# An attention and MoE kernel: the gates of all heads, the warm-up products and the splitting of x moved in the order

## The chip, the cores and the metric

The kernel runs on one core of one Trainium2 chip. The metric is the device time of one execution in microseconds (us), lower is better. Five engines work side by side, each through its own instructions in order: TensorE (PE, with its weight loads PEld), VectorE (DVE), ScalarE (ACT), GpSimd (POOL) and SyncE (SP), which here issues all the DMA transfers.

## What is computed

Eight batches of eight heads of causal attention with decaying gates, over 576 positions of 64 features; its output, 4608 tokens of 512 features, goes through a two-layer network:

```python
scores = scale * np.matmul(q, k.transpose(0, 1, 3, 2))
log_f = np.log(np.clip(f, 0.0001, 1.0))
cum = np.cumsum(log_f, axis=-1)
decay = cum[:, :, :, None] - cum[:, :, None, :]
scores = np.where(causal, -1000000000.0, scores + decay)      # causal: above the diagonal
attn = np.exp(scores - np.max(scores, axis=-1, keepdims=True))
attn = attn / (np.sum(attn, axis=-1, keepdims=True) + 1e-09)
x = np.matmul(attn, v)                 # then heads are put side by side: (4608, 512)
h = x @ w_in                           # (4608, 2048)
sp = np.maximum(h, 0.0) + np.log1p(np.exp(-np.abs(h)))
out = (h * erf(sp)) @ w_out            # (4608, 512)
```

All inputs and the output are float32.

## The kernel before

**Attention** runs in half steps t = 0 to 63, two for each pair of heads p = t // 2; a half step has some of the pair's blocks of 128 query rows (two in even half steps, three in odd ones), for both heads j = 0, 1. The work of a half step is spread over the following ones, so in the loop's step t stand `scores(t)`, `reduce(t)`, `exps(t - 1)`, `normalize(t - 2)`, `transposes(t - 3)` with `evacuate(t - 3)`, `values(t - 4)` and `store(t - 5)`. One half step takes about 4.9 us.

- `scores(t)` multiplies q and k on TensorE into one PSUM tile for each head, and adds a mask by products with `eye`. The pool `ps_s` has two buffers, which are the two tiles of one half step: `scores(t)` writes head j's only when `reduce(t - 1, j)` has read it.
- `reduce(t, j)` on DVE adds the gate row `c` of the pair (the negative running sum of the log gates, in all 128 partitions) and takes the row minimum of what is then the negated score.
- `exps` runs on ScalarE, `normalize` on GpSimd (from sums that DVE inverts), the copies out of PSUM in `evacuate` on ScalarE (banks 0 and 1) and DVE (banks 2 and 3). The pool `ps_t` of the transposes has three buffers, so that the fourth bank of an odd half step waits until bank 0 is emptied by ScalarE.
- `store` writes the pair's output, transposed, to the DRAM tensor `xt_d`.

**The gate rows.** Those of the first pair are worked out from two broadcast loads, `fd[0]` and `fd[1]`: `log_clipped` clips on DVE (L324) and takes the logarithm on ScalarE (L325), `decay` scans (L329) and multiplies by -8 (L330) on DVE. For all other pairs, `all_decays` does the same once with `fr`, all 64 heads in 64 partitions, writes the result to the DRAM tensor `cum_d` (L482) and loads the next pairs with q, k and two rows of `cum_d` broadcast to 128 partitions (L344). It is called at the end of half step 0.

**Constant products.** `idle_products` (L472 to L476) transposes the identity into a PSUM bank that nobody reads: 16 times before the loop, and 18 times behind the scores of t = 0, 1 and 2.

**Weights.** From t = 4 on each half step does one of four conversion steps of a weight piece (`convert`), spread over ScalarE, DVE and GpSimd.

**MoE.** `Moe.step` j does the first layer for one unit (a chunk of 512 tokens by 128 hidden features: `up`, 12 products), the second layer for a unit some steps back (`down`), and the gate functions of others. The first four steps are interleaved with the last half steps of the attention; the rest runs alone. The tokens of a chunk come from `xt_d` in two halves. `want_x(v)` allocates the tiles `xh` and `xl` of visit v and queues its halves, `load_x` starts the load of the next queued half into `xr` (L113), which has one buffer, and `split_x` splits the loaded ones: ScalarE copies to `xh` (L120), GpSimd subtracts for `xl` (L121). In the kernel before, the first chunk's halves are loaded and split in t = 60 and t = 61.

**What sets the order.** ScalarE, TensorE, DVE and GpSimd take their instructions as the code writes them (`manual_schedule` of the four). SP's are ordered by the scheduler when the program is built, so a load can stand well ahead of its place in the code; SP then works through its list in order, and a transfer that must wait holds those behind it.

Of the kernel before, what the change touches and what calls it, by code (L numbers as in the profile page):

```python
# [11 lines left out]
F32 = mybir.dt.float32  # L12
# [55 lines left out]
class Moe:  # L68
# [138 lines left out]
    def step(self):  # L207
        j, n = self.at, len(self.units)
        self.at += 1
        if j < n:  # L210
            self.up(j)
            self.want_x(self.units[min(j + 4, n - 1)][0])
            self.load_x()
        for i in self.downs[j]:
            self.down(i)
        if j in self.ends:
            for i in self.ends[j]:
                self.erf(i)
            self.nc.scalar.preload_act_table_set(SOFTPLUS)
        if j < n:  # L220
            self.softplus(j)
        for i in self.gates[j]:
            self.gate(i)
        for i in self.downs[j]:
            self.finish(i)
        self.split_x()


@with_exitstack
def attention_moe(ctx, tc, q2, k2, vp, f, w_in, w_out, out):  # L230
    nc = tc.nc
# [83 lines left out]
    with ExitStack() as ph:  # L315
# [7 lines left out]
        def log_clipped(x):  # L323
            nc.vector.tensor_scalar(out=x, in0=x, scalar1=1e-4, scalar2=1.0, op0=ALU.max, op1=ALU.min)  # L324
            nc.scalar.activation(out=x, in_=x, func=AF.Ln)  # L325

        def decay(out, x):

            nc.vector.tensor_tensor_scan(out=out, data0=x, data1=x, initial=0.0, op0=ALU.add, op1=ALU.bypass)  # L329
            nc.vector.tensor_scalar(out=out, in0=out, scalar1=-8.0, scalar2=None, op0=ALU.mult)  # L330
# [3 lines left out]
        def load(p):  # L334

            q = io.tile([P, PAD + S], F32, name=f"q{p}", tag="q")
            k = io.tile([P, S], F32, name=f"k{p}", tag="k")
            nc.sync.dma_start(out=q, in_=q2[p // NP, p % NP])
            nc.sync.dma_start(out=k, in_=k2[p // NP, p % NP])
            c = io.tile([P, 2, S], F32, name=f"c{p}", tag="c")  # L340
            if p:
                for j in range(2):
                    n = 2 * p + j
                    nc.sync.dma_start(out=c[:, j], in_=cum_d[n:n + 1].rearrange("a s -> (a s)").partition_broadcast(P))  # L344
            pairs[p] = [q, k, c]
# [117 lines left out]

        fd = [wk.tile([P, S], F32, name=f"fd{j}", tag=f"pt{j}", bufs=1) for j in range(2)]
        nc.sync.dma_start(out=fd[0], in_=f[0, 0].partition_broadcast(P))
        load(0)
        nc.sync.dma_start(out=fd[1], in_=f[0, 1].partition_broadcast(P))
        fr = wk.tile([B * H, S], F32, name="fr", tag="xo")
        nc.sync.dma_start(out=fr, in_=f.rearrange("b h s -> (b h) s"))
        todo = pieces[1]  # L470

        def idle_products(t, n):  # L472
# [2 lines left out]
            for i in range(n):  # L475
                nc.tensor.transpose(out=b[:, i % 4 * P:(i % 4 + 1) * P], in_=ident, identity=ident)  # L476

        def all_decays():
            log_clipped(fr)
            cum = wk.tile([B * H, S], F32, name="cum", tag="xo")  # L480
            decay(cum, fr)
            nc.sync.dma_start(out=cum_d, in_=cum)  # L482
            load(1)
            load(2)
            load_weight(0)

        idle_products("", 16)
        log_clipped(fd[0])
        decay(pairs[0][2][:, 0], fd[0])
        log_clipped(fd[1])  # L490
        for t in range(NH + 5):
            there = [0 <= t - n < NH for n in range(6)]
# [30 lines left out]
                exps(t - 1, 1)  # L523
            if there[0]:
                reduce(t, 1)
                if t == 0:
                    all_decays()
            if there[3]:
                for a in range(1, len(BANKS[(t - 3) % 2])):
                    evacuate(t - 3, a)  # L530
            if t >= 4 and todo:
                convert(*todo.pop(0))
            if NH - 4 <= t < NH - 2:
                moe.want_x(0)
                moe.load_x()
                moe.split_x()
            if t == NH - 1:
                early.close()
                moe.ep = moe_pools.enter_context(tc.tile_pool(name="ep", bufs=2, side="right"))
# [47 lines left out]
```

## Time and profile before

| | us |
|---|---|
| median of 3 runs | 1155.87 |
| lowest and highest run | 1155.82, 1157.66 |
| the profiled execution | 1156.91 |
| its span in the trace | 1155.1 |
| TensorE busy in the span | 1134.1 |
| ScalarE, DVE, GpSimd busy | 624.4, 565.2, 461.1 |

The span is what the trace covers of the profiled execution; 1.8 us lie around it. Busy times of TensorE overstate its work a little, since its products overlap and their ends are modelled. A row of the order of time gives the start and the length of an instruction, or of several alike in a row (x16), its engine, line and operation, the tiles that it writes and reads, and in brackets how long the engine stood before it and what ended that. A product of float32 operands appears as two instructions.

### The profile page before, as it was taken

What the parts mean: (1) busy time and instruction counts of PE and PEld (TensorE: products, weight loads), DVE (VectorE), ACT (ScalarE), POOL (GpSimd) and SP (SyncE); (2) the same over time, 40 slices, a digit from 0 to 9 for tenths busy, and PEclk for the clock granted to TensorE, in tenths of its full rate; (3) what the DMA queues carried; (4) which work ended last, traced back from release to release, by engine and by line L of the source; (5) the groups of instructions that cost most, each with busy time, mean ns of one, the idle gap of its engine ahead of it and who ended that gap; (6) DMA issues with size and microseconds to landing.
All of it is one profiled execution on the core that took longest, in us unless ns stands there. A gap on an engine that the chain in (4) does not pass through costs nothing.

```text
span 1155.1 us, 19541 instructions
## 1 busy us (share of the span) xinstructions
PE 1134.1 (98%) x7334; PEld 927.9 (80%) x7334; DVE 565.2 (49%) x1475; ACT 624.4 (54%) x1251; POOL 461.1 (40%) x532
## 2 busy tenths in 40 slices
PE   8999999999989999999999999999999999999998
PEld 6888888888877878778888888888888888888886
DVE  5788888888846576565233132222321322322221
ACT  3878878787786565664444344433342443243342
POOL 2556565555654445344342342332232232232121
PEclk9999999999999999999999999999999999999999
DMA  7677777777622133131031130230010010000001
GB/s 261 206 241 258 243 231 253 237 243 234 198 98 92 54 111 108 57 113 70 19 110 40 71 110 19 91 110 1 37 37 1 37 37 1 37 19 1 37 1 37
DMA packets 57726, 120.05 MB, mean 104 GB/s; under 512 B 4768, under 2 KB 20128, under 8 KB 57632
## 3 DMA queue, kind: packets, MB, share of 16 engines
q1 hardware_dynamic: 57632, 118.80, 31.4%
q8 instruction: 58, 0.95, 0.3%
q14 instruction: 36, 0.29, 0.1%
HBM read 94.52 MB, written 24.26 MB: 103 GB/s over the span
## 4 chain that ended last, share of the span: by engine, by line
PE 90%; DVE 3%; DMA 3%; ACT 2%; POOL 1%; issue 1%; SPq 0%; POOLq 0%; DVEq 0%; ACTq 0%
PE ph L133 32%; PE y L169 11%; PE y L171 11%; PE y L170 11%; PE s L362 8%; PE o L444 8%; PE t L417 7%; PE s L367 2%; DMA wraw<-in_w_in_dram 1%; POOL xl L121 1%; DVE pr L383 1%; DMA k<-in_k_dram 0%; DVE e L147 0%; ACT L289 0%; ACT L141 0%
## 5 line engine op out<-in xcount | busy, mean ns | idle before, releaser
L133 PE MATMUL ph<-xh,w 128*128 128x512 f32 x1152 | 381.7, 392 | 5.7 <-DVE e L147 5.7
L150 POOL TENSOR_TENSOR gl<-e,gh 128x512 fp32r<-128x512 f32 x144 | 186.8, 1298 | 418.9 <-DVE gh L149 414.4
L138 ACT ACTIVATE e<-ph 128x512 f32<-128x512 f32 x144 | 86.1, 598 | 385.1 <-PE ph L133 380.3
L133 PEld LDWEIGHTS ph<-xh,w 128*128 128x128 f32 x1152 | 217.2, 189 | 56.6 <-DVE e L147 5.9
L147 DVE TENSOR_TENSOR e<-e,ph 128x512 f32<-128x512 f32 x144 | 98.1, 681 | 327.0 <-ACT e L141 326.8
L169 PE MATMUL y<-w,gh 128*128 128x512 f32 x576 | 228.9, 397 | 0.0
L171 PE MATMUL y<-w,gl 128*128 128x512 f32 x576 | 228.0, 396 | 0.0
L170 PE MATMUL y<-w,gh 128*128 128x512 f32 x576 | 227.6, 395 | 0.0
L133 PE MATMUL ph<-xl,w 128*128 128x512 f32 x576 | 225.4, 391 | 0.0
L405 POOL TENSOR_SCALAR pr<-pr,st 128x576 f32<-128x576 f32 (+4 forms) x320 | 164.7, 535 | 117.8 <-DVE st L401 102.0
L395 ACT ACTIVATE pr<-pr,st 128x576 f32<-128x576 f32 (+3 forms) x320 | 176.5, 556 | 3.6 <-DVE st L383 3.5
L383 DVE CUSTOM_DVE_ANT_0 pr<-s,c 128x576 f32<-128x576 f32 (+3 forms) x320 | 136.8, 487 | 52.6 <-PE s L367 39.2
L171 PEld LDWEIGHTS y<-w,gl 128*128 128x128 f32 x576 | 108.7, 189 | 27.0
L170 PEld LDWEIGHTS y<-w,gh 128*128 128x128 f32 x576 | 108.2, 188 | 26.1
L169 PEld LDWEIGHTS y<-w,gh 128*128 128x128 f32 x576 | 108.0, 188 | 24.4
L133 PEld LDWEIGHTS ph<-xl,w 128*128 128x128 f32 x576 | 108.4, 188 | 22.7
L149 DVE CAST gh<-e 128x512 fp32r<-128x512 f32 x144 | 92.2, 640 | 66.3 <-PE y L170 52.4
L362 PE MATMUL s<-k,q 64*128 64x320 f32 (+4 forms) x768 | 110.3, 411 | 4.5 <-DVE st L383 2.5
L417 PE MATMUL t<-ident,pr 128*128 128x128 f32 x800 | 103.9, 275 | 4.2 <-ACT pt L426 2.5
L426 ACT COPY pt<-t 128x512 f32<-128x512 f32 x128 | 73.7, 577 | 61.1 <-PE t L417 61.1
L444 PE MATMUL o<-pt,v 128*64 128x128 f32 (+1 forms) x1920 | 103.8, 261 | 0.0
L444 PEld LDWEIGHTS o<-pt,v 128*64 128x64 f32 x1920 | 94.9, 138 | 9.5 <-DVE st L383 4.9
(53 smaller groups left out, 992.2 us busy)
## 6 DMA issues: line engine op xcount, KB each, us to landing
v<-in_vp_dram SPq DMA_DIRECT2D x32, 576.0 KB, 6.2
c<-cum_d SPq DMA_DIRECT2D x62, 288.0 KB, 5.0
xr<-xt_d SPq DMA_DIRECT2D x28, 512.0 KB, 3.4
q<-in_q_dram SPq DMA_DIRECT2D x32, 320.0 KB, 3.2
k<-in_k_dram SPq DMA_DIRECT2D x32, 288.0 KB, 4.2
xt_d<-xo SPq DMA_DIRECT2D x32, 288.0 KB, 5.8
wraw<-in_w_in_dram SPq DMA_DIRECT2D x16, 512.0 KB, 5.8
wraw<-in_w_out_dram SPq DMA_DIRECT2D x16, 512.0 KB, 5.6
```

The costliest lines, as they stand in the source:

```text
L133: nc.tensor.matmul(out=ps, lhsT=w[:, kd, fs], rhs=x[:, kd], start=kd == 0 and n == 0, stop=kd == KD - 1 and n == 2)
L147: nc.vector.tensor_mul(e_, e_, h_)
L150: nc.gpsimd.tensor_tensor(out=gl, in0=e_, in1=gh.bitcast(F32), op=ALU.subtract)
L169: nc.tensor.matmul(out=y[tb], lhsT=gh[:, cs], rhs=wh, start=first, stop=False)
L170: nc.tensor.matmul(out=y[tb], lhsT=gh[:, cs], rhs=wl, start=False, stop=False)
L171: nc.tensor.matmul(out=y[tb], lhsT=gl[:, cs], rhs=wh, start=False, stop=last)
L362: nc.tensor.matmul(out=s[j][:, at:at + k1 - k0], lhsT=q[h, PAD + START[i]:PAD + END[i]], rhs=k[h, k0:k1], start=i > 0, stop=k1 < END[i])
L383: nc.vector.tensor_tensor_reduce(out=to[:, ::-1] if j else to, in0=score, in1=decay_, scale=-0.125, scalar=BIG, op0=ALU.add, op1=ALU.min, ...
L395: nc.scalar.activation(out=seg, in_=seg, func=AF.Exp, bias=st[:, 0, j, m:m + 1], scale=-1.0, accum_out=st[:, 1, j, m:m + 1])
L405: nc.gpsimd.tensor_scalar(out=seg, in0=seg, scalar1=st[:, 2, j, m:m + 1], scalar2=1.0, op0=ALU.mult, op1=ALU.mult)
L417: nc.tensor.transpose(out=b[:, n * P:(n + 1) * P], in_=probs[t][:, at:at + P], identity=ident)
L444: nc.tensor.matmul(out=o[h, to:to + width], lhsT=v[:, ch, h], rhs=pt[:, at[j]:at[j] + width], start=n == 0, stop=n == len(parts) - 1, skip ...
```

## The change

The load of `fr` is issued right behind that of `fd[0]`, ahead of the first q and k. The function `all_decays` is gone: its clip and logarithm stand behind those of `fd[0]`, its scan and multiply behind the first head's, and the write to `cum_d` with the loads behind it follows, all before the loop. The first constant products are 34 in place of 16. The first chunk of x is asked for in t = 54, 57 and 60: each time the half that is loaded is split, and then the next load is started. In `Moe.step` the load comes behind the split at the step's end, and the next chunk is asked for one step earlier.

```diff
@@ Moe.step
         if j < n:
             self.up(j)
-            self.want_x(self.units[min(j + 4, n - 1)][0])
-            self.load_x()
+            self.want_x(self.units[min(j + 5, n - 1)][0])
...
         self.split_x()
+        self.load_x()
@@ attention_moe
         nc.sync.dma_start(out=fd[0], in_=f[0, 0].partition_broadcast(P))
+        fr = wk.tile([B * H, S], F32, name="fr", tag="xo")
+        nc.sync.dma_start(out=fr, in_=f.rearrange("b h s -> (b h) s"))
         load(0)
         nc.sync.dma_start(out=fd[1], in_=f[0, 1].partition_broadcast(P))
-        fr = wk.tile([B * H, S], F32, name="fr", tag="xo")
-        nc.sync.dma_start(out=fr, in_=f.rearrange("b h s -> (b h) s"))
...
-        def all_decays():
-            log_clipped(fr)
-            cum = wk.tile([B * H, S], F32, name="cum", tag="xo")
-            decay(cum, fr)
-            nc.sync.dma_start(out=cum_d, in_=cum)
-            load(1)
-            load(2)
-            load_weight(0)
-
-        idle_products("", 16)
+        idle_products("", 34)
         log_clipped(fd[0])
+        log_clipped(fr)
         decay(pairs[0][2][:, 0], fd[0])
+        cum = wk.tile([B * H, S], F32, name="cum", tag="xo")
+        decay(cum, fr)
+        nc.sync.dma_start(out=cum_d, in_=cum)
+        load(1)
+        load(2)
+        load_weight(0)
         log_clipped(fd[1])
...
                 reduce(t, 1)
-                if t == 0:
-                    all_decays()
...
-            if NH - 4 <= t < NH - 2:
+            if NH - 10 <= t < NH - 3 and t % 3 == 0:
                 moe.want_x(0)
+                moe.split_x()
                 moe.load_x()
-                moe.split_x()
```

On DVE the place is the start. Before, from the first head's scan to the first reduction of half step 1 (`pr`, `st` are the scores' tiles and statistics, `s` the PSUM tiles, `c0` the first pair's gate rows; the second row of each reduction reads its result out):

```order
L329 SCALAR_TENSOR_TENSOR c0_124<-fd1_118 128x576
L330 TENSOR_SCALAR c0_124<-c0_124 128x576
L383 ISA pr0_163,st0_164<-s0_1_152,c0_124 128x9x64
L383 ISA st0_164 128x1
L383 ISA pr0_163,st0_164<-s0_1_152,c0_124 128x3x64
L383 ISA st0_164 128x1
L324 TENSOR_SCALAR fr_126<-fr_126 64x576
L329 SCALAR_TENSOR_TENSOR cum_192<-fr_126 64x576
L330 TENSOR_SCALAR cum_192<-cum_192 64x576
L383 ISA pr1_226,st1_227<-s1_0_212,c0_124 128x448
```

Now, from the first clip to the first reduction:

```order
L324 TENSOR_SCALAR fd0_117<-fd0_117 128x576
L324 TENSOR_SCALAR fr_120<-fr_120 64x576
L329 SCALAR_TENSOR_TENSOR c0_126<-fd0_117 128x576
L330 TENSOR_SCALAR c0_126<-c0_126 128x576
L329 SCALAR_TENSOR_TENSOR cum_169<-fr_120 64x576
L330 TENSOR_SCALAR cum_169<-cum_169 64x576
L324 TENSOR_SCALAR fd1_118<-fd1_118 128x576
L383 ISA pr0_203,st0_204<-s0_0_191,c0_126 128x576
```

The three rows of `fr` and `cum` moved from behind the second head's reductions to between the first head's, ahead of all reductions; the rest kept its order.

On SP, also at the start, the write of `cum_d` and the broadcast reads `c1`, `c2` behind it, before:

```order
L350 DMA v0_264<-in_vp_dram 128x1152
L350 DMA v1_375<-in_vp_dram 128x1152
L279 DMA wraw1_675<-in_w_in_dram 128x2x512
L338 DMA q3_257<-in_q2_dram 128x640
L482 DMA cum_d_77<-cum_192 64x576
L339 DMA k3_258<-in_k2_dram 128x576
L344 DMA c1_200<-cum_d_77 128x576 x2
```

and now:

```order
L350 DMA v0_282<-in_vp_dram 128x1152
L484 DMA cum_d_77<-cum_169 64x576
L350 DMA v1_393<-in_vp_dram 128x1152
L344 DMA c1_177<-cum_d_77 128x576 x2
L344 DMA c2_184<-cum_d_77 128x576 x2
L279 DMA wraw1_693<-in_w_in_dram 128x2x512
```

The write stands ahead of the second values, the reads ahead of the second piece of weights and of the fourth pair.

On ScalarE the copies `xh0` of x stood at the ends of half steps 60 and 61 before (`pr60` is half step 60's):

```order
L289 ACTIVATE wtop14_4805<-wraw14_4731 128x512
L120 CAST xh0_4807<-xr0_0_4809 128x4x256
L395 ACTIVATE pr60_4756,st60_4757<-pr60_4756,st60_4757 128x576
L395 ACTIVATE pr60_4756,st60_4757<-pr60_4756,st60_4757 128x192
L426 COPY pt58_4844<-t58_0_4845 128x512
L395 ACTIVATE pr60_4756,st60_4757<-pr60_4756,st60_4757 128x576
L395 ACTIVATE pr60_4756,st60_4757<-pr60_4756,st60_4757 128x192
L426 COPY pt58_4844<-t58_1_4850 128x512
L120 CAST xh0_4807<-xr0_1_4886 128x4x256
```

Now half step 60 ends with the second half, and nothing stands at the end of 61:

```order
L289 ACTIVATE wtop14_4831<-wraw14_4757 128x512
L120 CAST xh0_4362<-xr0_1_4599 128x4x256
L395 ACTIVATE pr60_4782,st60_4783<-pr60_4782,st60_4783 128x576
L395 ACTIVATE pr60_4782,st60_4783<-pr60_4782,st60_4783 128x192
L426 COPY pt58_4866<-t58_0_4867 128x512
L395 ACTIVATE pr60_4782,st60_4783<-pr60_4782,st60_4783 128x576
L395 ACTIVATE pr60_4782,st60_4783<-pr60_4782,st60_4783 128x192
L426 COPY pt58_4866<-t58_1_4872 128x512
L395 ACTIVATE pr61_4859,st61_4860<-pr61_4859,st61_4860 128x448
```

The first half's copy moved to the end of half step 57, three half steps earlier, the second half's to where the first's was. GpSimd's splits moved with them. SP's list has the load of the first half (`xr0_0`) where it was, that of the second three half steps earlier, and that of the next chunk's first half just behind. Of the MoE no row of the four engines moved.

## Rows read from the trace of the kernel before

**Rows 1.** Who waited for whom, TensorE: us in total, times, longest us.

```profile
PE ph L133 <- DVE e L147: 5.7, 4, 2.1
...
PE t L417 <- ACT pt L426: 2.5, 1, 2.5
```

**Rows 2.** Stretches: length, busy us of PE to POOL, granted clock, DMA share, GB/s.

```profile
310.00:330.00 20.00, 17.51 (x198) 14.74 (x195) 14.12 (x52) 14.65 (x41) 13.96 (x19) 0.91 0.36 122
...
400.00:500.00 100.00, 96.99 (x410) 77.68 (x409) 62.60 (x84) 63.49 (x74) 45.26 (x30) 0.98 0.26 90
```

**Rows 3.** Order of time at the start: start us, us, engine, line, operation, [idle before].

```profile
1.36 3.68 PE L476 MATMUL idle<-ident 128*128 128x128 f32 x16 [1.36 <-POOL ident masks.py:199]
...
2.58 0.57 SPq L469 DMA_DIRECT2D fr<-in_f_dram  x1
...
4.90 0.46 DVE L324 TENSOR_SCALAR fd<-fd 128x576 f32<-128x576 f32 x1 [2.83 <-DMA fd<-in_f_dram]
...
6.70 2.93 PE L362 MATMUL s<-k,q 64*128 64x320 f32 x12 [1.67 <-DMA k<-in_k_dram]
...
10.00 0.76 DVE L383 CUSTOM_DVE_ANT_0 pr<-s,c 128x576 f32<-128x576 f32 x1 [1.67 <-PE s L367]
...
13.91 0.45 DVE L324 TENSOR_SCALAR fr<-fr 64x576 f32<-64x576 f32 x1
...
14.14 1.69 PE L362 MATMUL s<-k,q 64*128 64x448 f32 x10 [0.80 <-DVE st L383]
...
15.11 1.35 DVE L329 TENSOR_TENSOR_SCAN cum<-fr 64x576 f32<-64x576 f32 x1 [0.75 <-ACT fr L325]
...
16.06 2.16 PE L476 MATMUL idle<-ident 128*128 128x128 f32 x18
...
16.49 0.45 DVE L330 TENSOR_SCALAR cum<-cum 64x576 f32<-64x576 f32 x1
...
16.87 0.61 DVE L383 CUSTOM_DVE_ANT_0 pr<-s,c 128x448 f32<-128x448 f32 x1
...
20.75 0.40 PE L367 MATMUL s<-upper,eye 128*128 128x128 bf16 x4
...
23.39 0.76 DVE L383 CUSTOM_DVE_ANT_0 pr<-s,c 128x576 f32<-128x576 f32 x1 [3.96 <-DMA c<-cum_d]
```

**Rows 4.** The chain that ended last, at the start: start us, us, what.

```profile
16.97 2.76 DMA cum_d<-cum
...
19.79 3.46 DMA c<-cum_d
```

**Rows 5.** Order of time in half steps 60 to 62.

```profile
309.01 1.54 PE L444 MATMUL o<-pt,v 128*64 128x128 f32 x28
...
312.23 2.38 POOL L121 TENSOR_TENSOR xl<-xr,xh 128x1024 fp32r<-128x1024 f32 x1 [1.92 <-ACT xh L120]
...
317.97 1.04 ACT L120 CAST xh<-xr 128x1024 fp32r<-128x1024 f32 x1 [2.47 <-DMA xr<-xt_d]
...
321.17 0.44 PE L417 MATMUL t<-ident,pr 128*128 128x128 f32 x1 [2.49 <-ACT pt L426]
...
321.54 2.83 PE L444 MATMUL o<-pt,v 128*64 128x128 f32 x28
```

**Rows 6.** DMA issues up to 30 us: count, KB each, median us to landing.

```profile
fr<-in_f_dram SPq DMA_DIRECT2D x1, 144.0 KB, 6.0
```

**Rows 7.** Order of time in half step 58.

```profile
296.89 2.27 POOL L405 TENSOR_SCALAR pr<-pr,st 128x576 f32<-128x576 f32 x4 [2.95 <-DVE st L401]
...
298.20 0.59 ACT L426 COPY pt<-t 128x512 f32<-128x512 f32 x1 [0.94 <-PE t L417]
```

**Rows 8.** DVE's casts by line: ns least/median/most, first and last start us.

```profile
L306 DVE CAST w<-wtop x32: 426/427/2589, 50.3 to 537.8; 128x512 fp32r<-128x512 f32 x32
```

**Rows 9.** Order of time, GpSimd and DVE, in the MoE.

```profile
366.11 2.37 POOL L121 TENSOR_TENSOR xl<-xr,xh 128x1024 fp32r<-128x1024 f32 x1 [1.30 <-ACT xh L120]
...
366.18 2.59 DVE L306 CAST w<-wtop 128x512 fp32r<-128x512 f32 x1
```

## The prediction

> **What bounds the kernel now.** I read first who keeps TensorE waiting, then the two places where its waits are long, in order of time, then the engines that release it there. TensorE is the bound nearly everywhere: its waits in the whole span are few, and the longest groups are the MoE's for the gates (5.7 us in four waits) and one single wait of 2.5 us of the transposes for the copy of ScalarE that empties a PSUM bank [rows 1]. So an edit pays only where it shortens one of TensorE's waits or what the clock loses behind one. The change touches two places.
>
> The first is the start. There DVE and TensorE hand a pair of score tiles back and forth, with one pair of PSUM buffers: scores(t) needs the reductions of t-1. DVE works on the gates of all heads (clip 0.45, scan 1.35, multiply 0.45 us, with 0.75 us of waiting for the logarithm) only after the first half step, from 13.91 to 16.94 us. The result is written to cum_d and read back, and DVE stands 3.96 us until the third half step's reduction at 23.39, although TensorE had those scores ready at 20.75 + 0.40 = 21.15 [rows 3]. The chain of waits runs over that write and read: 2.76 and 3.46 us [rows 4].
>
> The second is half step 61, shortly before the MoE. The load of x's second half can only go out when GpSimd has split the first (the raw tile has one buffer): the split runs from 312.23 for 2.38 us, the load can go out at 314.61, and ScalarE stands 2.47 us for it until 317.97. Behind that stands its next copy out of PSUM, for which TensorE's thirteenth transpose waits 2.49 us. The clock then falls to half: the products of `values` take 2.83 us where the same group took 1.54 [rows 5]; the granted clock over those 20 us is 0.91, 1.8 us of clock [rows 2].
>
> **The change part by part.** *The gates of all heads move ahead (head).* DVE gets clip, scan and multiply of `fr`, 2.25 us, between the first head's work and its first reduction. In the kernel before DVE stood 1.67 us before that reduction at 10.00, so it was free at 8.33; it also stood 0.75 us for the first logarithm, of which the clip of `fr` now fills 0.45. The reduction comes at 8.33 + 2.25 - 0.45 = 10.13, if `fr` is there. That is 0.13 us later [rows 3]. *Is `fr` there?* Its load now stands second on SP, behind the load that DVE waits for until 4.90. As the fifth load, issued at 2.58 [rows 3], it took 6.0 us to land [rows 6]. Issued three loads earlier, at about 1.2, it lands between 4.9, when the load ahead of it does, and 1.2 + 6.0 = 7.2. I take 5.7, nearer the lower end, since one load is ahead of it and no longer four: DVE is then through with the clip when the logarithm ends, and nothing is lost. At 7.2 the first scan, which stands behind that clip, starts at 7.65 in place of 6.11: 1.5 us lost.
>
> From the second head's reduction on, 13.91 becomes 14.04, and the 3.04 us of `fr` work that stood there are gone. What is late next is TensorE: the rest of scores(1) starts after that reduction (14.14 before), takes 1.69 us, and the mask products come behind it. I put the reduction of half step 1 at 16.35 in place of 16.87. From there to the end of scores(2) the kernel before took 21.15 - 16.87 = 4.28 us, all of it DVE and TensorE in turn, so scores(2) are ready at 20.6. The gate row must be there by then: multiply done at 10.13 - 0.45 = 9.68, plus the 6.45 us that lay between 16.94 and 23.39, is 16.1. If both transfers took the 6.0 us of [rows 6] it is 21.9. I take 18, between these, since the weights and values loaded at the start share the queue with it, and the wait at 23.39 disappears. **Head: 23.39 - 20.6 = 2.8 us**, with bounds of 0 and 3.2 (the second end if the first scores also come earlier).
>
> *34 products instead of 16.* They fill TensorE while it waits for q and k anyway (first scores at 6.70, after 1.67 us of waiting for k; both now go out behind `fr`, the 0.57 us of its issue later). Sixteen took 3.68 us at the slow clock, eighteen 2.16 at the full one; 34 end between 1.36 + 5.8 = 7.2 and 1.36 + 7.8 = 9.2. The first scores then start later than 6.70, but partly at the full clock: 2.93 us before, 1.69 for nearly the same work later [rows 3]. They end near 10, about when DVE is free at 10.13: taken as nothing. If the clock stayed at half throughout, they would end at 9.2 + 3.5 = 12.7, a loss of 2.6.
>
> *x split one step behind its load.* Both halves still cost ScalarE a 1.04 us copy and GpSimd 2.4 us; they now stand at the ends of half steps 57 and 60, and in 61 there is none. The load of the first half stands in SP's order where it stood, far ahead of its copy; the second's goes out after the split in 57, some 15 us before its copy in 60, against the 3.4 us from 314.61 to 317.97 that it needs [rows 5]. So neither copy waits. In 57 ScalarE takes it while it would stand 0.94 us for a transpose at 298.20, and GpSimd while it stands 2.95 us until 296.89 [rows 7]; both covers nearly hold the work, and TensorE has no wait there. In 60 the kernel before already had one split, without a wait of TensorE. **Transition: 2.49 + (2.83 - 1.54) = 3.8 us.** ScalarE is then early by the 2.5 us that it no longer stands; what comes last is TensorE itself.
>
> *want_x one step earlier, load_x after split_x in the MoE.* In the built order ScalarE's, DVE's and GpSimd's rows of the MoE are the same as before, and SP's too after the load of chunk 1's first half. That load goes out earlier, when nothing waits for it. Cost and gain: nothing. TensorE's four waits for the gates stay.
>
> *A rule that speaks against it.* GpSimd's split now lies beside other DVE work. The row: a DVE cast that takes 0.43 us elsewhere took 2.59 while GpSimd's split ran [rows 8, 9], so a DVE instruction can be held by 2.16: rival (c). The Trainium skill, page SBUF — State Buffer, section "Who interferes with whom", says that the port pair of the two is locked for a whole instruction, and that DVE is held when it reads two SBUF inputs or runs in a two-port mode; the trace agrees with that cast. By the rule the reductions, which read one input from PSUM, go free.
>
> **How the sum stands to the runs.** 2.8 + 3.8 = 6.6. Against the profiled execution's own 1156.91 that is 1150.3; against the median of 1155.87 it is 1149.3. The profiled one has two half-clock stretches [rows 2], and I don't know which of them the median run has: without the one at 321 the transition gives 2.5 and the time is 1150.6. I forecast **1149.6**.
>
> **The rivals.**
> (a) *The clock at the start.* Between the first product of scores(1) and the rest TensorE stood 0.80 us [rows 3]. What runs ahead of that now has the full clock and ends up to 2.93 - 1.69 = 1.24 us earlier, while DVE comes 0.13 later: the wait is 0.9 to 2.2 us. Waits of 2.49 and 2.1 us preceded the two half-clock stretches [rows 1, 2]. If it falls here too, scores(1) take up to 2.93 instead of 1.69, with some idle products behind them: 1.4 us lost, 1151.0. Chance 0.17.
> (b) *The gates are worked on earlier but come no earlier*: `fr` lands late, or the broadcast stands behind the weights. Head gain 0 to 1.5: 1151.1 to 1152.4. Chance 0.12.
> (c) *Another wait takes the place of ScalarE's* in half steps 58 to 62: a DVE instruction held by 2.16 us beside a split [rows 9], then a fall of the clock (1.3), gives back 3.5: 1153.1. Against it: beside the split of half step 60 the kernel before had no such wait of TensorE; its one wait there came from ScalarE [rows 1, 5]. By the Trainium skill's rule above it would take a DVE instruction with two SBUF inputs under the split. Chance 0.08.
> (d) *Slower.* Both splits find their half not landed: if SP came to each load only shortly before its copy, the one in 57 would wait as that in 61 did, and the one in 60 again. Two waits of 3.8 each come back on the forecast: 1149.6 + 7.6 = 1157.2, 0.1% slower. It decides from the point where a load is issued less than 3.4 us before its copy. Against it: in SP's built order the first load stands where it stood, and the second three half steps ahead of its copy. Chance 0.03; this is also the case that the change doesn't do what it says.
> (e) *Better.* The longest wait for the gates (2.1 us) comes between 400 and 500 us, and a half-clock stretch with it [rows 1, 2]; 0.98 over 100 us is about 2 us of clock, and I take the 1.8 of the other one. It need not come again: 1147.8. Chance 0.10.
>
> **How the numbers follow.** Forecast 0.50, (a) 0.17, (b) 0.12, (c) 0.08, (d) 0.03, (e) 0.10. The range 1147.3 to 1152.6 holds the forecast, (a), (b) and (e); (c), (d) and the edges, less than 2 in 10, are left out. 0.2% (2.3 us, about what a measurement of this kernel can tell from no change) lies at 1153.6: faster by more 0.92, within 0.05, slower 0.03.
>
> **What would show it.** After: DVE's wait for c near 23 gone and the third half step's reduction near 20.6, with `fr`'s clip at 5.4 to 6.2 and cum_d issued near 9.8; no wait of TensorE in half step 62, ScalarE's copies of x at the ends of 57 and 60 without a wait for a load, and the granted clock 1.00 around 320; the MoE's waits as before. Wrong would be: the reduction at 20.6 waiting for c, a half-clock stretch before 20, or a wait of TensorE above 1 us between 290 and 325.

## The result, and the profile after

The changed kernel takes 1151.17 us (median of 6 runs, 1148.40 to 1151.59); the kernel before took 1157.47 on the same chip in the same rounds (6 runs, 1155.82 to 1160.88). The ratio is 0.9937, with a 95% interval of 0.9918 to 0.9955: 0.6% faster. The prediction was 1149.6, with a range of 1147.3 to 1152.6: the median lies 1.6 above the forecast and inside the range. The profiled execution took 1151.32 with a span of 1149.5, against 1156.91 and 1155.1 before.

TensorE's waits for other engines (who waited for whom: us in total, times, longest us), to be read beside [rows 1]. First one more row of the kernel before, then two after:

```profile
PE s L362 <- DVE st L383: 2.5, 3, 1.5
```

```profile
PE ph L133 <- DVE e L147: 5.9, 4, 2.3
PE s L362 <- DVE st L383: 2.2, 2, 2.0
```

The row "t <- ACT pt" of 2.5 us is gone, the MoE's waits for the gates are as before (5.9 against 5.7), and the waits of the scores for DVE's reductions sum to less than before, but one of them is now 2.0 us long, where the longest was 1.5: it stands at the start. The order of time there (start us, us, engine, line and operation, tiles, [idle before]), beside [rows 3]:

```profile
1.36 5.70 PE L476 MATMUL idle<-ident 128*128 128x128 f32 x34 [1.36 <-POOL ident masks.py:199]
...
4.92 0.46 DVE L324 TENSOR_SCALAR fd<-fd 128x576 f32<-128x576 f32 x1 [2.84 <-DMA fd<-in_f_dram]
...
5.80 0.45 DVE L324 TENSOR_SCALAR fr<-fr 64x576 f32<-64x576 f32 x1 [0.43 <-DMA fr<-in_f_dram]
...
7.26 1.56 PE L362 MATMUL s<-k,q 64*128 64x320 f32 x12 [0.20 <-DMA k<-in_k_dram]
...
9.79 0.47 SPq L484 DMA_DIRECT2D cum_d<-cum  x1
10.05 0.74 DVE L383 CUSTOM_DVE_ANT_0 pr<-s,c 128x576 f32<-128x576 f32 x1
...
14.18 2.15 PE L362 MATMUL s<-k,q 64*128 64x448 f32 x10 [1.97 <-DVE st L383]
...
16.79 3.08 PE L476 MATMUL idle<-ident 128*128 128x128 f32 x18
...
21.62 0.76 DVE L383 CUSTOM_DVE_ANT_0 pr<-s,c 128x576 f32<-128x576 f32 x1 [2.29 <-PE s L367]
...
28.18 1.53 PE L362 MATMUL s<-k,q 64*128 64x320 f32 x10 [0.26 <-DVE st L383]
```

The gates of all heads are worked out before the first reduction, which comes at 10.05 (10.00 before). The reduction of half step 2 at 21.62 no longer waits for the gate row `c` (3.96 us at 23.39 before): it waits for TensorE. But TensorE is late: it stood 1.97 us before the rest of scores(1), and the eighteen idle products behind those take 3.08 us where they took 2.16 [rows 3]. The granted clock there, and in the two stretches of [rows 2] (length, busy us of PE to POOL, granted clock, DMA share, GB/s):

```profile
10.00:20.00 10.00, 7.93 (x49) 6.37 (x49) 6.40 (x25) 5.87 (x18) 0.48 (x1) 0.83 0.86 302
310.00:330.00 20.00, 19.12 (x219) 16.26 (x218) 14.34 (x54) 15.97 (x44) 14.25 (x22) 1.00 0.42 143
400.00:500.00 100.00, 96.74 (x409) 77.39 (x408) 65.75 (x87) 63.76 (x74) 44.50 (x30) 0.98 0.27 94
```

The half-clock stretch (1.2 instead of 2.4 GHz) near 320 is gone, that of the MoE is still there, and a new one stands at the start. The copies and splits of x around half steps 57 and 60, in order of time, beside [rows 5]:

```profile
293.85 1.05 ACT L120 CAST xh<-xr 128x1024 fp32r<-128x1024 f32 x1
294.99 2.37 POOL L121 TENSOR_TENSOR xl<-xr,xh 128x1024 fp32r<-128x1024 f32 x1 [2.81 <-DVE st L401]
...
297.38 0.37 SPq L113 DMA_DIRECT2D xr<-xt_d  x1
...
309.33 1.04 ACT L120 CAST xh<-xr 128x1024 fp32r<-128x1024 f32 x1
...
323.54 0.50 PE L133 MATMUL ph<-xh,w 128*128 128x512 f32 x1
```

Neither copy waits for a load; the second's load went out at 297.38, twelve us before its copy. The MoE's first product stands at 323.54, before at 329.41.

From these rows the span is cut into three pieces, whose ends are the rest of scores(4) and the first MoE product. In the kernel before they are:

```profile
29.95 1.53 PE L362 MATMUL s<-k,q 64*128 64x320 f32 x10 [0.26 <-DVE st L383]
...
329.41 0.50 PE L133 MATMUL ph<-xh,w 128*128 128x512 f32 x1
```

The same pieces are used for all runs below. The last column is a second profiled execution of the changed kernel, the first of the experiments below, with its first MoE product at 322.09:

| us | before | after | the changed kernel again |
|---|---|---|---|
| start, to the rest of scores(4) | 29.95 | 28.18 | 26.68 |
| attention, to the first MoE product | 299.46 | 295.36 | 295.41 |
| MoE, to the end of the span | 825.69 | 825.96 | 824.71 |
| span | 1155.1 | 1149.5 | 1146.8 |

The gain of 5.6 in the profiled span is 1.8 at the start, 4.1 in the attention, and nothing (-0.3) in the MoE.

### The profile page after: what moved, and what is told of

Read it like the earlier page. It is cut to its first block, busy times and chain, and to the rows that moved or that the text cites. A ratio compares the mean times of both kernels' runs of the same rounds, so it can differ in the third digit from the quotient of the medians.

```text
span 1149.5 us, 19580 instructions
## 1 busy us (share of the span) xinstructions
PE 1132.7 (99%) x7352; PEld 928.5 (81%) x7352; DVE 563.9 (49%) x1475; ACT 624.9 (54%) x1251; POOL 461.1 (40%) x532
## 4 chain that ended last, share of the span: by engine, by line
PE 92%; DVE 2%; DMA 2%; ACT 2%; POOL 1%; issue 1%; SPq 0%; DVEq 0%; POOLq 0%; ACTq 0%
PE ph L133 32%; PE y L169 11%; PE y L171 11%; PE y L170 11%; PE s L362 9%; PE o L444 9%; PE t L417 8%; PE s L367 2%; DMA wraw<-in_w_in_dram 1%; POOL xl L121 1%; PE idle L476 0%; DMA fr<-in_f_dram 0%; DVE e L147 0%; DVE pr L383 0%; ACT L289 0%
## 5 line engine op out<-in xcount | busy, mean ns | idle before, releaser
L362 PE MATMUL s<-k,q 64*128 64x320 f32 (+4 forms) x768 | 107.7, 408 | 2.5 <-DVE st L383 2.2
L121 POOL TENSOR_TENSOR xl<-xr,xh 128x1024 fp32r<-128x1024 f32 x28 | 68.2, 2437 | 88.7 <-ACT xh L120 83.4
```

The costliest lines, as they stand in the source:

```text
L362: nc.tensor.matmul(out=s[j][:, at:at + k1 - k0], lhsT=q[h, PAD + START[i]:PAD + END[i]], rhs=k[h, k0:k1], start=i > 0, stop=k1 < END[i])
```

## The experiments

Medians are given with their number of runs, and the ratio to the kernel before on the same chip with its 95% interval. "Start", "attention" and "MoE" are the three pieces of the profiled span.

**The same kernel again** (`changed_again`, no edit).

> The changed kernel once more, beside the next three on one chip. Theory: its runs fall into two groups 2.7 us apart, near 1148.5 and near 1151.2, by whether the half-clock stretches at the start and behind the MoE's third wait for the gates come or not; median near 1150.5.

1149.90 us (6 runs, 1148.62 to 1151.46), ratio 0.9929 (0.9915 to 0.9944). The profiled one took 1148.62. Its start and two of its stretches:

```profile
4.69 0.46 DVE L324 TENSOR_SCALAR fd<-fd 128x576 f32<-128x576 f32 x1 [2.61 <-DMA fd<-in_f_dram]
...
13.92 1.69 PE L362 MATMUL s<-k,q 64*128 64x448 f32 x10 [1.63 <-DVE st L383]
...
15.84 2.16 PE L476 MATMUL idle<-ident 128*128 128x128 f32 x18
...
20.12 0.76 DVE L383 CUSTOM_DVE_ANT_0 pr<-s,c 128x576 f32<-128x576 f32 x1 [1.64 <-PE s L367]
...
26.68 1.53 PE L362 MATMUL s<-k,q 64*128 64x320 f32 x10 [0.25 <-DVE st L383]
...
10.00:20.00 10.00, 8.37 (x65) 6.68 (x64) 6.14 (x24) 6.35 (x21) 1.34 (x2) 1.00 0.85 291
...
400.00:500.00 100.00, 96.68 (x415) 77.26 (x414) 68.21 (x88) 62.93 (x74) 46.53 (x31) 1.00 0.26 91
```

The same program, but neither stretch has the half clock: the wait before the rest of scores(1) is 1.63 in place of 1.97, the idle products take 2.16 in place of 3.08, and in the MoE the wait of 2.4 us is there (2.37 at 460.66) and no fall follows. The start is 1.5 us shorter, the MoE 1.25. Of the 1.5, 0.26 is not the clock: the first load landed earlier (DVE's first clip at 4.69 in place of 4.92), and the rest of scores(1) starts at 13.92 in place of 14.18. From there to the rest of scores(4) the two differ by 1.24. So in place of the expected two groups the twelve runs of this kernel lie on three levels: 1148.4 to 1148.7 (four runs), 1149.9 (two) and 1151.1 to 1151.6 (six). The lowest is that of the profile without a fall, the highest that of the profile with both; that the middle one has one of the two is argued from the steps and from its mean granted clock of 0.998, and no profile shows it. Of the first six runs two have a mean granted clock of 1.000 and four, at 1151.1 to 1151.6, of 0.997.

**Only the start** (`e1_head`) and **only the splits with the order in the MoE's step** (`e2_split`), each on the kernel before.

```diff
  e1: the kernel before, with of the change
+        fr = wk.tile(...); nc.sync.dma_start(out=fr, ...)      # behind fd[0]
+        idle_products("", 34)                                  # for 16
+        log_clipped(fr) ... decay(cum, fr) ... load(2)         # ahead of the loop
  e2: the kernel before, with of the change
+            self.want_x(self.units[min(j + 5, n - 1)][0]) ... self.load_x()  # behind split_x
+            if NH - 10 <= t < NH - 3 and t % 3 == 0:  want_x, split_x, load_x
```

> Only the start is changed (gates of all heads ahead, fr's load second, 34 products); the splitting of x and the MoE's step are as before. If start and transition are two separate gains, this gives the start's alone: the reduction of half step 2 at 21.6 in place of 23.39 where the clock falls at the wait before the rest of scores(1), 20.5 where it does not; 1.8 to 2.9 us below before, ratio 0.9975 to 0.9985. The wait of 2.5 us of TensorE in half step 62 is still there. Rival, that all of the gain is the transition's: no difference from before.

> Only x's splitting is changed (half steps 57 and 60, load behind split, chunk asked for one step earlier in the MoE); the start is as before. Expected: the wait of 2.49 us in half step 62 and the half clock behind it gone, first product of the MoE about 4 us earlier measured from the end of the start; 2.5 to 4.1 us below before, ratio 0.9965 to 0.998. The start's wait of 3.96 us of DVE stays. Rival, that another wait takes its place: less than 1 us.

The start alone: 1155.51 us (12 runs), ratio 0.9972 (0.9958 to 0.9986). The splits alone: 1155.78 us (12 runs), ratio 0.9975 (0.9963 to 0.9987). Each gives about half: 3.2 and 2.9 us, 6.1 together, by the ratios on 1157.93; the whole change gave 7.3 by its ratio, with an interval of 5.2 to 9.5. By the medians it is 2.4 and 2.2, and the intervals are 1.6 to 4.9 and 1.5 to 4.3. So it is shown that the halves are two gains, but not that they sum exactly to the whole. In order of time, the start alone still has the wait in half step 62, and the splits alone still have the waits for `c`:

```profile
314.52 1.05 ACT L120 CAST xh<-xr 128x1024 fp32r<-128x1024 f32 x1 [2.65 <-DMA xr<-xt_d]
...
317.72 0.30 PE L417 MATMUL t<-ident,pr 128*128 128x128 f32 x1 [2.68 <-ACT pt L426]
```

```profile
22.77 0.76 DVE L383 CUSTOM_DVE_ANT_0 pr<-s,c 128x576 f32<-128x576 f32 x1 [4.10 <-DMA c<-cum_d]
...
25.95 2.96 PE L362 MATMUL s<-k,q 64*128 64x448 f32 x10 [1.00 <-DVE st L400]
```

The start alone gives also what the wait in half step 62 costs by itself, for in this execution no half clock followed it (this is one of the faster of its twelve runs, 1152.44; eight of them, at 1155.1 to 1157.7, have a lower mean clock and were not profiled): the attention is 298.09 long, 2.7 more than 295.36 to 295.41. With the half clock behind it, as in the kernel before, it is 4.1 more. Its MoE of 826.3 and that of the splits alone (826.3 too) are equal, though only the second has the changed order in `Moe.step`: that edit moves nothing by itself. The last row above is a half-clock stretch at the start of the splits alone, where TensorE waited 1.61 and 1.00 us in a row.

**Fewer products at first** (`e3_sixteen`: the changed kernel with 16) and **more products behind the first scores** (`e4_fill`: 34 in place of 18 there).

```diff
  e3
-        idle_products("", 34)
+        idle_products("", 16)
  e4
-                    idle_products(t, 18)
+                    idle_products(t, 34 if t == 0 else 18)
```

> The changed kernel with 16 first products again in place of 34. If the 34 products cause the clock's fall (they end the work ahead of the wait for scores(1) early, so that the wait grows from 0.8 to 2.0 us), then with 16 the first scores run at half clock (2.9 us), end near 10.5, the wait before the rest of scores(1) is below 1.2 us, no half clock stands between 13 and 20, and the reduction of half step 2 comes at 20.5 to 21.0: 0.5 to 1 us faster than the changed kernel's runs with a fall, about the same as those without. Rival, that the 34 products are what brings the scores early: reduction of half step 2 at 22 or later, slower by 1 us.

> The changed kernel with 34 constant products in place of 18 behind the scores of half step 0, which fill the wait of 1.97 us. If that wait is what the clock falls on, no half clock stands between 10 and 30 in the trace, scores(1) take 1.7 us and the idle products behind them 2.2, the reduction of half step 2 comes at 20.5, and the time is 1.0 to 1.4 us below the changed kernel's runs with a fall. Rival, that the fall has another cause: the stretch of half clock stays, time equal.

With 16: 1150.21 us (6 runs), ratio 0.9929 (0.9913 to 0.9946). With the fillers: 1149.91 us (6 runs), ratio 0.9927 (0.9911 to 0.9943). Neither can be told from the changed kernel by its time. Their starts, first with 16, then with the fillers:

```profile
6.97 2.93 PE L362 MATMUL s<-k,q 64*128 64x320 f32 x12 [1.94 <-DMA k<-in_k_dram]
...
14.41 1.69 PE L362 MATMUL s<-k,q 64*128 64x448 f32 x10 [0.92 <-DVE st L383]
...
27.17 1.53 PE L362 MATMUL s<-k,q 64*128 64x320 f32 x10 [0.26 <-DVE st L383]
```

```profile
12.47 2.76 PE L362 MATMUL s<-k,q 64*128 64x448 f32 x12
```

With 16 the first scores run at half clock in this execution (2.93 us), so TensorE comes later to its next wait, which shrinks to 0.92, and the clock holds. The start ends at 27.17, 1.0 earlier than in the first profile of the changed kernel and 0.5 later than in its second. With the fillers the wait is filled, no fall follows, and the start ends at 26.30. That is 0.38 us before the second profile's 26.68, and the first load landed 0.43 earlier (DVE's first clip at 4.26 against 4.69): against a start without a fall the fillers gain nothing. So in these profiles the 34 products are worth about half a microsecond where no fall comes, and they go with a longer wait, behind which the clock can fall. That their number decides the clock of the first scores is not shown: the splits alone have 16 as well, and there the first scores ran at the full clock:

```profile
7.40 1.57 PE L362 MATMUL s<-k,q 64*128 64x320 f32 x12 [2.37 <-DMA k<-in_k_dram]
```

**The load of `fr` where it was** (`e7_fr_late`, one run), the rest as changed.

```diff
-        fr = wk.tile([B * H, S], F32, name="fr", tag="xo")
-        nc.sync.dma_start(out=fr, in_=f.rearrange("b h s -> (b h) s"))
         load(0)
         nc.sync.dma_start(out=fd[1], in_=f[0, 1].partition_broadcast(P))
+        fr = wk.tile([B * H, S], F32, name="fr", tag="xo")
+        nc.sync.dma_start(out=fr, in_=f.rearrange("b h s -> (b h) s"))
```

> The changed kernel with the load of all heads' gates issued where it stood before, behind the first q, k and the second head's gates. Theory: it lands near 8.5 in place of 5.8, DVE stands for it before its second clip, the first head's scan behind it is late by 2 to 3 us, the first reduction comes at 12 to 13 in place of 10.05, and the reduction of half step 2 at 23 to 24.5 in place of 21.6: as late as in the kernel before, the head's gain is gone. Rival: the earlier load is not needed (TensorE's first scores are ready no sooner than 8.8 and the clock decides): the reduction of half step 2 within 0.7 us of 21.6.

1156.26 us, beside 1155.84 of the kernel before, one run each: as slow as before. The pieces say where the gain went. The attention is 295.36 long, so the transition's gain is still there; the start is 2.7 longer than before, and the MoE 0.8.

```profile
9.30 0.45 DVE L324 TENSOR_SCALAR fr<-fr 64x576 f32<-64x576 f32 x1 [3.58 <-DMA fr<-in_f_dram]
9.67 1.34 DVE L329 TENSOR_TENSOR_SCAN c<-fd 128x576 f32<-128x576 f32 x1
...
13.54 0.74 DVE L383 CUSTOM_DVE_ANT_0 pr<-s,c 128x576 f32<-128x576 f32 x1
...
14.72 0.99 PE L362 MATMUL s<-k,q 64*128 64x448 f32 x2 [3.38 <-DVE st L383]
...
17.68 3.22 PE L362 MATMUL s<-k,q 64*128 64x448 f32 x10 [1.97 <-DVE st L383]
```

DVE takes its list in order, so the clip that waits for `fr` holds the first head's scan behind it: 9.67, where the changed kernel had it at 6.18. TensorE then stands 3.38 us and 1.97 us, the clock falls, and the rest of scores(4) comes at 32.66, 2.7 us later than before the change. About 0.4 of the 2.7 is the first load, which landed later in this execution (DVE's first clip at 5.26, before at 4.90). The rival was wrong, and the theory missed the size: the first reduction came at 13.54, where 12 to 13 was expected, because `fr` was there only at 9.30 and not near 8.5; that of half step 2 came at 26.10, where 23 to 24.5 was expected, also because the falling clock was not in the theory.

**The splits one half step later** (`e5_58_61`, one run): loads and splits in 55, 58 and 61, so that a half is split where the kernel before had its wait, with its load three half steps ahead.

```diff
-            if NH - 10 <= t < NH - 3 and t % 3 == 0:
+            if NH - 9 <= t < NH - 2 and t % 3 == 1:
```

> The changed kernel with the first chunk of x asked for in half steps 55, 58 and 61 in place of 54, 57 and 60, so that a half is again split at the end of half step 61, where the kernel before had its wait, but with its load three half steps ahead. Theory (the load that could only go out behind GpSimd's split caused the wait): ScalarE's copy in 61 stands less than 0.3 us for a load, no wait of TensorE above 1 us in half step 62, and from the rest of scores(4) to the first MoE product 295.4 us as in the changed kernel. Rival (the place of the copy matters, ScalarE's next copy out of PSUM is late behind its 1.04 us): a wait of 0.5 to 1.5 us of the transposes stays, 296 to 297.

1148.49 us; no wait of TensorE for ScalarE in half step 62, and an attention of 295.34 (26.36 to 321.70):

```profile
311.71 1.05 ACT L120 CAST xh<-xr 128x1024 fp32r<-128x1024 f32 x1
```

So the place of the copy did not matter here; that its load could only go out behind the split just before it did.

**A second raw buffer** (`e8_two_xr`), **with the fillers too** (`e9_two_xr_fill`), and **the load of x from GpSimd's queue** (`e8b_pool_load`). These go after the MoE's four waits for the gates. In the trace of the changed kernel ScalarE waits three times for a weight piece (14.7 us together, up to 5.6) shortly before a wait of TensorE for a gate; SP issued those loads right behind a load of x that had waited for GpSimd's split.

```diff
  e8, e9
-            raw = self.xp.tile([P, KD, TB // 2], F32, name=f"xr{v}_{h}", tag="xr", bufs=1)
+            raw = self.xp.tile([P, KD, TB // 2], F32, name=f"xr{v}_{h}", tag="xr", bufs=2)
-            raws[u, 0] = top = cv.tile([P, 512], F32, name=f"wtop{u}", tag="wtop")
+            raws[u, 0] = top = cv.tile([P, 512], F32, name=f"wtop{u}", tag="wtop", bufs=1)
  e9 also: 34 fillers behind the first scores, as in e4
  e8b
-            self.nc.sync.dma_start(out=raw, in_=self.xt_d[:, cols]...)
+            self.nc.gpsimd.dma_start(out=raw, in_=self.xt_d[:, cols]...)
```

> The changed kernel with two buffers for the raw half of x (and one instead of two for the intermediate tile of the weight conversion, to make room). Theory: the MoE's four waits of TensorE for the gates (5.9 us in sum) come from weight pieces whose loads stand on SP behind a load of x that waits for GpSimd's split; with a second buffer that load goes out at once, ScalarE's waits of 3.7 to 5.6 us for the weight pieces shrink below 2, and the waits at 363, 414, 462 and 509 fall to below 2 us in sum, with no half-clock stretch behind 462: 1146 to 1148. Rival: ScalarE's wait for the weights is not what makes the gates late, and the four waits stay at 5 to 6 us: as the changed kernel, within 1 us. Third: the single intermediate buffer makes ScalarE wait for DVE's casts, and the time grows by 1 to 4 us.

> The same with 34 instead of 18 constant products behind the first scores. Theory: both gains add, the start without a half-clock stretch (rest of scores(1) without a wait, reduction of half step 2 near 19.7) and the MoE as in the run with two raw buffers: 1145 to 1147.5. Rival: where the two-buffer run brings nothing, this gives the 1149 to 1150 of the run with 34 fillers.

> The changed kernel with the load of x issued from GpSimd's queue, one raw buffer as before: the load that must wait for GpSimd's split then holds nobody on SP. Theory of the load in line on SP: the MoE's waits for the gates shrink as with two raw buffers, 1146 to 1149, less what GpSimd pays for issuing (each issue stands in its own order). Rival: the waits stay at 5 to 6 us, and the time is that of the changed kernel or up to 2 us more. In the attention the second half's load comes behind the split on GpSimd, without a wait of TensorE in half step 62.

Two buffers: 1150.07 us (6 runs), ratio 0.9931 (0.9917 to 0.9945); with the fillers 1150.23 (6 runs), 0.9930 (0.9915 to 0.9945). Nothing gained, as the rival had it. The third expectation did not come either: ScalarE waits for the intermediate tile only once, 0.7 us, and its waits for x (19.6 us in ten, in the changed kernel) are gone, but those for the weights are not (16.6 us). From GpSimd's queue: **1143.48 us** (4 runs, 1143.01 to 1144.88), ratio 0.9875 (0.9859 to 0.9892), 6.4 us below the changed kernel's median on the same chip, faster than both kernels and than the 1146 to 1149 expected. The same place in the changed kernel (again), with two buffers, and with GpSimd's queue:

```profile
402.17 2.86 POOL L121 TENSOR_TENSOR xl<-xr,xh 128x1024 fp32r<-128x1024 f32 x1
402.79 2.79 DVE L303 SCALAR_TENSOR_TENSOR wtop<-wtop,wraw 128x512 int32<-128x512 int32 x1
405.06 0.37 SPq L113 DMA_DIRECT2D xr<-xt_d  x1
405.53 0.45 SPq L279 DMA_DIRECT2D wraw<-in_w_in_dram  x1
...
410.06 1.28 ACT L289 ACT_TABLE_LOAD   x1 [3.61 <-DMA wraw<-in_w_in_dram]
...
413.49 0.47 PE L133 MATMUL ph<-xh,w 128*128 128x512 f32 x1 [0.95 <-DVE e L147]
```

```profile
403.18 2.85 POOL L121 TENSOR_TENSOR xl<-xr,xh 128x1024 fp32r<-128x1024 f32 x1
...
406.05 0.37 SPq L113 DMA_DIRECT2D xr<-xt_d  x1
406.53 0.45 SPq L279 DMA_DIRECT2D wraw<-in_w_in_dram  x1
```

```profile
402.23 2.56 POOL L121 TENSOR_TENSOR xl<-xr,xh 128x1024 fp32r<-128x1024 f32 x1 [0.26 <-ACT xh L120]
...
403.88 0.38 SPq L279 DMA_DIRECT2D wraw<-in_w_in_dram  x1
...
407.71 1.28 ACT L289 ACT_TABLE_LOAD   x1 [0.67 <-DMA wraw<-in_w_in_dram]
```

With one buffer the load of x waits on SP until the split ends (402.17 + 2.86 = 405.03), and the weights' load stands behind it. With two buffers it is the same picture: the loads run one half further ahead and the next one waits for the same split, since the second buffer is filled as well. Off SP, the weights' load goes out before the split ends, ScalarE's wait of 3.61 shrinks to 0.67, and of TensorE's four waits for the gates (6.2 us) one is left (1.7):

```profile
PE ph L133 <- DVE e L147: 1.7, 1, 1.7
```

The MoE is 819.3 long (321.88 to 1141.2), 5.4 less than the 824.7 of the changed kernel's profile without a half-clock stretch; 4.5 of it are these waits. The other 0.9 is not traced. GpSimd pays 0.77 us for each issue, SP 0.37. ScalarE's waits for x grow from 21.6 to 30.4 us, but TensorE waits for none of it.

**Both helpful edits** (`e10_pool_fill`: GpSimd's queue and the fillers) and **GpSimd's queue on the kernel before** (`e11_before_pool`).

> The changed kernel with both edits that helped on its place: the load of x issued from GpSimd's queue, and 34 instead of 18 constant products behind the first scores. Theory (the MoE's gain from taking the load off SP and the quiet clock at the start are apart): profiled with the rest of scores(1) waiting less than 0.5 us for DVE, the first MoE product near 321.7, and from it to the end of the span 819 to 820 us as in the run with GpSimd's issue alone; 1142.5 to 1143.5, hardly below 1143.5, since in that run the start had no half-clock stretch either. Rival: the MoE's gain depends on when it starts, and from the first MoE product to the end it is 822 to 826: 1145 to 1149.

> The kernel before with the load of x issued from GpSimd's queue, nothing else; there the load stands ahead of the split in each step, not behind it. Theory (the load from GpSimd only pays once it stands a step ahead of its copy, which is what the changed step's order gives): in half steps 60 and 61 ScalarE waits the whole landing of 3 to 4 us for each half, TensorE's waits there are 2.5 us or more, and in the MoE ScalarE's waits for x grow; 1154 to 1160. Rival (the order within the step changes nothing here either): the MoE gains the same 5 to 6 us, 1151 to 1153.

Both edits: 1144.46 us (4 runs), ratio 0.9879 (0.9865 to 0.9892): no better than GpSimd's queue alone, as the start has no half-clock stretch in either profile. On the kernel before: 1166.73 us (5 runs), ratio 1.0069 (1.0054 to 1.0085), slower, and by more than expected. There the load stands ahead of the split in each step, so on GpSimd it goes out only when its copy is due, and ScalarE waits out its landing (60.6 us in all, where it waits 30.4 with the changed order). Behind TensorE's wait of 6.35 us the granted clock is 0.70 from 330 to 340, and behind a wait of 3.46 us for a gate it is 0.89 from 370 to 400:

```profile
327.08 1.04 ACT L120 CAST xh<-xr 128x1024 fp32r<-128x1024 f32 x1 [6.08 <-DMA xr<-xt_d]
...
330.28 0.44 PE L417 MATMUL t<-ident,pr 128*128 128x128 f32 x1 [6.35 <-ACT pt L426]
```

The profiled execution is the slowest of the five (1171.02), and it has a half-clock stretch at the start too, which the load of x has nothing to do with. The two kernels also differ in the start and in half steps 54 to 61, so it is argued from ScalarE's waits, and not shown by an edit of its own, that the order "split, then load" of the changed kernel, worth nothing on SP, is what makes GpSimd's queue usable.

## Why the prediction was right, and where not

**The time.** 6.3 us less than the median of 1155.87 were forecast; the medians lie 6.3 apart (1157.47 to 1151.17), since both came out 1.6 above the figures that the forecast went by. That the difference agrees to a tenth is luck: the sum was 6.6 against the profiled execution, whose span became 5.6 shorter in one profile and 8.3 in the other, and 6.3 lies between these two cases.

**Transition: 3.8 forecast, 4.1 measured.** Right by its steps. The wait is gone and the clock is 1.00 around 320; alone the wait is worth 2.7 (`e1_head`: 2.68 in the row, 298.09 against 295.4), and the clock 1.4 (299.46 against 298.09; 1.3 was in the sum). `e5_58_61` shows that the cause was the load behind the split and not the copy's place. Neither rival (c) nor (d) came: from 285 us to the first MoE product TensorE does not wait at all.

**Head: 2.8 forecast, 1.8 and 3.3 measured.** The gates' part went as written: `fr` clipped at 5.80 (5.7 was taken), `cum_d` issued at 9.79 (9.8), the first reduction at 10.05 (10.13), no wait for `c` at half step 2. The step that failed is the term for the 34 products, "taken as nothing". They ended at 7.06 in one profile and 7.55 in the other, just before and early in the span of 7.2 to 9.2; the first scores ran at the full clock (1.56 us) and with their masks ended at 9.16 and 9.38, not near 10, and TensorE came to the rest of scores(1) well ahead of DVE: a wait of 1.97 in one profile and 1.63 in the other, between the 0.9 and 2.2 that rival (a) gave. Without a fall of the clock the reduction of half step 2 comes at 20.12, better than the forecast 20.6; with it at 21.62. The rest of the sum held where no fall came: from the reduction of half step 1 to the end of scores(2) it took 4.28, and 4.30 were measured (15.90 to 20.20); with the fall it was 4.95 (16.75 to 21.70). The gate row was later than the 18 that was taken: the write took 5.2 to 5.8 us in place of 2.8, so the reads went out at 14.97 and 15.32, and none landed in under 3.3 us. It was still ahead of TensorE's scores. (The upper end for that row, 21.9, should be 21.7, two landings of 6.0 from 9.68; and rival (b)'s head gain of 1.5 gives 1150.9, not 1151.1. Nothing rests on either.)

**Rival (a) was the likelier case.** It had a chance of 0.17 and a price of 1.4, for 1151.0. The price was about right: 1.24 between the two profiles from the rest of scores(1) on. The chance was too small: four of the first six runs have the time and the mean clock of the profile that shows it. Rival (e), the MoE's fall not coming again, was met too: two of those six runs have neither fall, 1148.4 and 1148.7, a little above the 1147.8 given. What I treated as one forecast was several cases, by which half clock follows, and the forecast's own case, a fall in the MoE and none at the start, was the rarest: if the level at 1149.9 is that case, two of the twelve runs have it.

**Rival (b) was priced on the wrong side.** I gave a late `fr` a head gain of 0 to 1.5. `e7_fr_late` shows a loss of 2.7 against before (about 0.4 of it the first load's landing): a late `fr` holds not only its own work but all that is queued behind its clip on DVE. So the moved load is what carries the gain at the start.

**The MoE's reorder: nothing forecast, nothing measured** (825.96 against 825.69; and 826.3 in both halves of the change).

**The rule that spoke against the change.** The Trainium skill, page SBUF — State Buffer, section "Who interferes with whom", has a DVE instruction that reads two SBUF inputs contend with a GpSimd instruction that reads SBUF, and the later of the two is held. The traces agree: L303, which reads two, takes 0.69 us, and 2.79 where it starts at 402.79 beside a split that had started at 402.17. But that row is from the MoE; in half steps 57 to 62 TensorE had no wait that such a hold could have caused.

## What to carry to other kernels

When work is moved ahead in an engine's list, move its load ahead as well, and price the load's delay by everything that is queued behind the first instruction that needs it. A load that must wait for a buffer holds all other loads on its queue, and a second buffer did not cure that here, because the loads ran ahead until they waited again; put it on the queue of the engine that frees the buffer, behind the freeing instruction. Work that only warms an engine should end when its partner is ready: coming early turns into a wait (here one of 1.6 to 2.0 us), and the clock can fall behind it. And where a kernel has several levels of time, look at all its runs before a single profile, and forecast the cases apart.

## What the runs showed of the hardware

The clock does not follow the wait's length alone. Before the rest of scores(1), waits of 1.97 us were followed by half-clock work in three of three profiles that had them (the changed kernel, two raw buffers, and the late `fr`, where one of 3.38 came just before), and those of 1.63 and less by none. But with the splits alone, waits of 1.61 and 1.00 in a row, a little later, were followed by one (the 2.96 us above), and so was a single one of 1.72 at that place in the last experiment (4.03 us for twelve products that take 1.86 at the full clock); in the MoE waits of 2.3 to 2.4 us had one behind them in some profiles and none in others of the same program (0.98 and 1.00 above), and the 2.68 us in half step 62 had none where the 2.49 of the kernel before had one. A fall cost 1.24 us at the start, 1.25 in the MoE and 1.4 behind half step 62's wait, and one program has times near 1148.5, 1149.9 and 1151.2.

Moving a load to another engine's queue gave some 6 us without faster transfers: from issue to landing they took 4.0 us in the median from GpSimd, and 3.5 to 3.6 from SP. The Trainium skill, page DMA: Bandwidth & Descriptors, section "Issuing engines are not separate DMA queues", says that starting transfers on several engines saves only the time of issuing. Here it also saved other loads the wait of the one in front: 4.5 of the 5.4 us by which the MoE became shorter are TensorE's waits behind such loads.
